# Centred tokens for the first gate chunks, earlier loads for slab 2, and a y tile between state inputs

## The chip, the cores and the metric

The kernel runs on one core of a Trainium2 chip. The time is device microseconds of that core for one execution; each version is run several times and its median is given. One more execution is taken with the hardware profiler, and everything called "the profile" or "the trace" comes from it.

The engines are named as the profile names them: PE (matrix products; PEld loads the stationary operand), DVE (vector operations), ACT (activation functions, also used to move results out of PSUM, the memory that PE writes to), POOL (here only powers and small copies) and SP (which issues nearly all DMAs, in order).

## What is computed

Tokens `x` (2048 of them, 512 channels, bf16) are layer-normalised. The normalised tokens feed two branches, a state space model with 512 complex states and a gated feed-forward network with 1376 hidden channels, and the branches are multiplied:

```python
xn = _layernorm(x, axis=-1)
# branch s: for each of 512 complex states
dt = jnp.exp(log_dt); Lam_bar = jnp.exp(dt * Lam)
B_bar = ((Lam_bar - 1.0) / Lam)[:, None] * Bmat
Bu = jnp.einsum("bld,pd->blp", xn + 0j, B_bar)
h = Lam_bar[None, :] * h + Bu[:, t, :]          # for t in range(2048)
s = 2.0 * jnp.einsum("blp,dp->bld", hseq, Cmat).real + xn * Dskip
# branch g
g = _silu((_gelu(xn @ w_gate) * (xn @ w_up)) @ w_down)
return x + s * g
```

## The kernel before, in words

**Tiling.** The 2048 tokens are four slabs (`s` = 0 to 3) of 512, each of four tiles (`m` = 0 to 3) of 128 tokens. A tile's normalised tokens `xn` must be turned (channels on the partitions) before PE can use them: `xnT`. For slab 0 PE turns them with an identity matrix (`head_t`, L427), and ACT (L430) or DVE (L432, tile 3) evicts the result; for the later slabs a DMA transpose does it (`dma_t`, L453).

**Work of a slab.** *Gate*: products of a tile with `wg` and `wu`, ACT takes Gelu of the one and copies the other, DVE multiplies them into `at`, and a DMA transpose turns that (`at_t`, L527). In slab 0 the weights come in three chunks of columns (`CH0`: 384, 512, 480), and `gate_pair` (L480 the products, L485 the copy `ub`, L486 the Gelu `gt`, L487 the product) takes one chunk of one tile; in the later slabs `gate_tile` (L501) takes a whole tile. *States*: `half(s, h)` has PE multiply the slab with two quarters of B (L612), ACT evicts to `U` (L615), and DVE rotates (L626, L634, L638), scans along time (L645) and rotates back into `hst`. *Down* (`down_pair`, L544): `atT` with `wd`, then ACT takes Silu into `g2` (L548). *y* (`y_tile`, L574): `hst` with `C2`, times `g2` (L578), plus the tokens (L586), stored to `out` (L589). The skip term `sk` (L457) is put into the y bank by ACT before the products (L570); for the first two y tiles only, DVE adds it behind the products instead (L582, L584).

**PSUM.** Three slots of two banks and two single banks (`ybank`). The gate pairs of chunk 0 take slots 0, 1, 2 and, for tile 3, both y banks; the first pair of chunk 1 is back at slot 0, so it must wait until pair 0 has been evicted by ACT.

**Order.** The steps are written down in a list (`Plan`), each with its engine, an estimated cost, the keys that it reads and writes, an earliest time and a rank. PE's order is the one written; DVE's is too while `in_turn` is set. For the other engines and queues a search (`run`) over orders of this list, with `TRIALS` random changes, takes the order that its estimates make shortest, and the instructions are issued in it. A wait on the chip comes from the keys alone. DMAs that are given with `dma_first` keep their order on their queue.

**The head, as it is written.** Stand-in products (`dummies`, L419, whose results nobody reads) run until there are tokens. Per tile of slab 0, DVE takes statistics (`stats`, L402), mean and variance (`mean`, L406), adds epsilon (`rstd`, L412), POOL raises that to -1/2 (`power`, L409), and DVE normalises (`norm_dve`, L444). In between, DVE makes the angles of the state tables (`angle`, L665 to L672). ACT loads its Sin table (L377) directly behind the Exp for `dt`, takes the two sines (L678, L679) and loads the Gelu table ahead of the first Gelu (L486). `spread` (L716, L717) copies Dskip to all partitions through slot 2, `damping` (L707) uses `ybank[0]`. SP's queue carries, in this order: tokens and weights of chunks 0 and 1, the tokens of slab 1 (L346), both parts of B turned (L348), the weights of chunk 2, `wd` (L753, L754), then slab 1's four turned tiles and both parts of C (L841; they land in `hst[1]`).

Of the kernel before, what the change touches and what calls it, by code (L numbers as in the profile page):

```python
# [19 lines left out]
LOOK, HOLD, TABLE, ROUNDS, TRIALS = 0.3, 8.0, 6.0, 6, 3000  # L20
# [182 lines left out]
def kernel(  # L203
# [50 lines left out]
    xnT = sb("xnT", [P, KT, 2 * TS])  # L254
# [20 lines left out]
    xn = [sb(f"xn{i}", [P, D]) for i in range(M)]  # L275
# [5 lines left out]
    tF = sb("tF", [P, 2, D], FP32)  # L281
    junk = sb("junk", [P, D])
# [31 lines left out]
    def dma_first(eng, issue, land, emit, writes, **kw):  # L314

        first[eng] = dma(eng, issue, land, emit, writes=writes, after=[first[eng]] if eng in first else (), **kw)
# [29 lines left out]
    dma_first(SP, 1.45, 4.0, lambda: nc.sync.dma_start(out=x_tok[:, M : 2 * M, :], in_=x_r[:, M : 2 * M, :]), [("x", 1, m) for m in range(M)])  # L346
    for ri, src in enumerate((A_B_re, A_B_im)):
        dma_first(SP, 2.4, 4.0, lambda ri=ri, src=src: nc.sync.dma_start_transpose(out=BT[:, ri, :, :], in_=src), [("BT", ri)])  # L348
    for which in range(2):
        load_w(dma_first, SP, nc.sync, 2, (1.35, 4.1), which)  # L350
# [21 lines left out]
    def columns():  # L372

        pe(1, 150, lambda: T.matmul(rows, lhsT=pv[0][:], rhs=ident[0 : 2 * NPT, 0 : 2 * NPT], start=True, stop=True),
            [("pv", 0), ("pv", 1), "ident"], [("slot", 2, 0)])
        acts(4, lambda: act(out=dt_, in_=rows[:, 0:NPT], func=AF.Exp), [("slot", 2, 0), "tiny"], ["dt"], table="exp", rank=150.0)
        acts(1, lambda: act(out=tiny[:], in_=zero[:], func=AF.Sin), ["zero", "dt"], ["tiny"], table="silu", rank=150.0)  # L377
# [44 lines left out]
    def transposed(src, n, dst, reads, writes, bank, evict):  # L422
        tp = ybank[bank][:].bitcast(BF16)[:, 0:D].rearrange("p (k t) -> p k t", t=P)

        def f():
            for k in range(KT):
                T.transpose(tp[:, k, :], src[:, k * P : (k + 1) * P], ident[:])  # L427
        pe(KT, P, f, reads + ["ident"], [("y", bank)])
        if evict == ACT:
            acts(512, lambda: act(out=dst, in_=tp, func=AF.Copy), [("y", bank)], writes, rank=100.0)  # L430
        else:
            dve(512, lambda: V.tensor_copy(out=dst, in_=tp), [("y", bank)], writes, rate=2.0, rank=40.0)  # L432
# [10 lines left out]
    def norm_dve(s, m):  # L443
        dve(512, lambda: V.tensor_scalar(  # L444
            out=xn[m][:], in0=x_tok[:, s * M + m, :], scalar1=mv[:, s, m, 0:1], scalar2=rs[:, s, m : m + 1],
            op0=ALU.subtract, op1=ALU.mult), [("x", s, m), ("mv", s, m), ("rs", s, m)], [("xn", m)], rate=2.0)

# [3 lines left out]
    def dma_t(s, m):  # L451
        c0 = (s % 2) * TS + m * P
        return dma(SP, 1.2, 4.5 if s == 1 else 1.3, lambda: nc.sync.dma_start_transpose(out=xnT[:, :, c0 : c0 + P], in_=xn[m][:]),  # L453
            [("xn", m)], turned_tile(s, m))

    def skip(s, m):
        dve(512, lambda: V.tensor_tensor(out=sk[s % 2][:, m, :], in0=xn[m][:], in1=Drow[:], op=ALU.mult),  # L457
            [("xn", m), "Drow"], [("sk", s % 2, m)], rate=2.0)
# [4 lines left out]
    def gate_pair(s, m, c, then=((), ()), spare=False):  # L463

        if spare:
            pss, both = [ybank[0][:], ybank[1][:]], [("y", 0), ("y", 1)]
        else:
            i, ps = slot()
            pss, both = [ps[:, 0, :], ps[:, 1, :]], [("slot", i, 0), ("slot", i, 1)]
        a, b = CH0[c]  # L470
        w = b - a
        j = (s * M + m) % NAT
        t0 = (s % 2) * TS + m * P
        q = gu_n[0] % (2 * NGT)
        gu_n[0] += 1
        qb, qo = q // 2, (q % 2) * 512
        for bank, (nm, wt) in enumerate((("wg", wg), ("wu", wu))):
            def f(bank=bank, wt=wt):
                for k in range(KT):
                    T.matmul(pss[bank][:, 0:w], lhsT=xnT[:, k, t0 : t0 + P], rhs=wt[:, k, a:b], start=(k == 0), stop=(k == KT - 1))  # L480
            pe(KT, w, f, turned_tile(s, m) + [(nm, c)], [both[bank]])
            for t in then[bank]:
                t()
        gd, ud = gt[qb][:, qo : qo + w], ub[qb][:, qo : qo + w]
        acts(w, lambda: act(out=ud, in_=pss[1][:, 0:w], func=AF.Copy), both, [("ub", q)])  # L485
        acts(w, lambda: act(out=gd, in_=pss[0][:, 0:w], func=AF.Gelu_apprx_tanh), both, [("gt", q)], table="gelu", after=early if c == 0 else (), rank=40.0 if c + m == 0 else 0.0)  # L486
        dve(w, lambda: V.tensor_tensor(out=at[j][:, a:b], in0=gd, in1=ud, op=ALU.mult), [("gt", q), ("ub", q)], [("at", j, c)], rate=2.0)  # L487

    def gate_tile(s, m):

        j = (s * M + m) % NAT
        t0 = (s % 2) * TS + m * P
# [3 lines left out]
        def mm(ps, bank, wt, c):  # L496
            a, b = CH[c]

            def f():
                for k in range(KT):  # L500
                    T.matmul(ps[:, bank, 0 : b - a], lhsT=xnT[:, k, t0 : t0 + P], rhs=wt[:, k, a:b], start=(k == 0), stop=(k == KT - 1))  # L501
# [51 lines left out]
    def y_tile(s, m):  # L553
        i = y_n[0] % 2
        seed = y_n[0] >= 2
# [7 lines left out]
        for bank, key, a, z in parts:  # L563
            y_part(s, m, bank, key, a, z, i, e, gi, b, seed)

    def y_part(s, m, bank, key, a, z, i, e, gi, b, seed):

        w = z - a
        if seed:
            acts(w, lambda: act(out=bank, in_=sk[s % 2][:, m, a:z], func=AF.Copy), [("sk", s % 2, m)], [key])  # L570

        def f():
            for j in range(2 * NPT):
                T.matmul(bank, lhsT=hst[s % 2][:, j // NPT, j % NPT, m * P : (m + 1) * P], rhs=C2[:, j // NPT, j % NPT, a:z],  # L574
                         start=(j == 0 and not seed), stop=(j == 2 * NPT - 1), skip_group_check=True)
        pe(2 * NPT, w, f, [("hst", s % 2, 0), ("hst", s % 2, 1)] + C2S + ([key] if seed else []), [key])
        if seed:
            dve(w, lambda: V.tensor_tensor(out=yg[e][:, a:z], in0=bank, in1=g2[gi][:, b, a:z], op=ALU.mult),  # L578
                [key, ("g2", gi)], [("yg", e, a)], base=0.13)
        else:  # L580
            ys = tF[:, i, :]
            dve(512, lambda: V.tensor_tensor(out=ys, in0=bank, in1=sk[s % 2][:, m, :], op=ALU.add),  # L582
                [key, ("sk", s % 2, m)], [("tF",)], base=0.13)
            dve(512, lambda: V.tensor_tensor(out=yg[e][:], in0=ys, in1=g2[gi][:, b, :], op=ALU.mult),  # L584
                [("tF",), ("g2", gi)], [("yg", e, a)], base=0.13)
# [16 lines left out]
    def half(s, h):  # L602

        ui = u_n[0] % NU
        u_n[0] += 1
        for q in range(H2):
            i, ps = slot()
            pt = h * H2 + q
            for ri in range(2):
                def f(ri=ri, pt=pt, ps=ps):  # L610
                    for k in range(KT):
                        T.matmul(ps[:, ri, :], lhsT=BT[:, ri, k, pt * P : (pt + 1) * P], rhs=xnT[:, k, (s % 2) * TS : (s % 2 + 1) * TS],  # L612
# [3 lines left out]
                 [("slot", i, 0), ("slot", i, 1)], [("U", ui, q)])  # L616
        WQ = [P, 2, 2, H2 * TS]
# [56 lines left out]
    def tables():  # L674
# [3 lines left out]
        early.append(acts(196, lambda: act(out=sbt[:], in_=ang[:], func=AF.Sin, scale=TWO_PI), ["ang"], ["sbt"], table="silu", rank=20.0))  # L678
        early.append(acts(196, lambda: act(out=cbt[:], in_=kr[:], func=AF.Sin, scale=-TWO_PI, bias=halfpi[:]), ["kr", "halfpi"], ["cbt", "trig"], table="silu", rank=20.0))  # L679
        for f32, lo, pr, n in ((cbt, ch, cp, "c"), (sbt, sh, sp, "s")):  # L680
            pool(0.5, lambda f32=f32, lo=lo: G.tensor_copy(out=lo[:], in_=f32[:, :, 0:NB]), [n + "bt"], [n + "h"])
            acts(128, lambda f32=f32, pr=pr: act(
                out=pr[:], in_=f32[:, :, NB : NB + NA].unsqueeze(3).to_broadcast([P, NPT, NA, 2]), func=AF.Copy), [n + "bt"], [n + "p"], rank=40.0)
# [28 lines left out]
    def head_t(m):  # L712
        transposed(xn[m], m, xnT[:, :, m * P : (m + 1) * P], [("xn", m)], [("xnT", 0, m)], m % 2, DVE if m == 3 else ACT)

    def spread():
        pe(1, 512, lambda: T.matmul(slots[2][:, 1, :], lhsT=warm[0:1, 0:P], rhs=Drow[0:1, :], start=True, stop=True), ["Drow", "warm"], [("slot", 2, 1)])  # L716
        acts(512, lambda: act(out=Drow[:], in_=slots[2][:, 1, :], func=AF.Copy), [("slot", 2, 0), ("slot", 2, 1)], ["Drow"])  # L717
# [3 lines left out]
    dummies(3, 0)  # L721
# [3 lines left out]
    rstd(0, 0, 1)  # L725
    stats(0, 1)
    mean(0, 1)
    norm_dve(0, 0)
    rstd(0, 1, 2)
    head_t(0)  # L730
    dummies(2, 0, 3)
    turn_angles()
    angle(0)
    norm_dve(0, 1)
    stats(0, 2)
    mean(0, 2)
    rstd(0, 2, 3)
    angle(1)
    stats(0, 3)
    norm_dve(0, 2)  # L740
    mean(0, 3)
    rstd(0, 3, 4)
    angle(2)
    angle(3)
    norm_dve(0, 3)
    pl.in_turn = False
    tables()
    then = {0: ((lambda: head_t(1), spread), ()), 1: ((lambda: head_t(2),), ()), 2: ((lambda: head_t(3),), ())}
    for m in range(M):
        gate_pair(0, m, 0, then.get(m, ((), ())), m == M - 1)  # L750
        if m == 1:
            damping()
    dma_first(SP, 3.6, 4.3, lambda: nc.sync.dma_start(out=wd[:, 0 : NFT - 1, :], in_=B_w_down[0 : (NFT - 1) * P, :].rearrange("(k p) d -> p k d", p=P)), ["wd"])  # L753
    dma_first(SP, 0.4, 4.3, lambda: nc.sync.dma_start(out=wd[:FL, NFT - 1, :], in_=B_w_down[(NFT - 1) * P : F, :]), ["wd"])  # L754
    for m in range(M):
        skip(0, m)
    for m in range(M):
        gate_pair(0, m, 1)
    for h in range(2):
        half(0, h)  # L760
    for m in range(M):
        gate_pair(0, m, 2)
# [38 lines left out]
    turned = {}  # L801

# [108 lines left out]
```

## Time and profile before

| what | us |
|---|---|
| median of 5 runs (lowest to highest) | 181.02 (180.85 to 181.15) |
| profiled execution | 181.15 |
| its span, first to last instruction | 179.4 |
| around the span | 1.75 |
| PE busy (share) | 173.5 (97%) |
| DVE busy | 158.1 (88%) |
| ACT busy | 117.4 (65%) |
| POOL busy | 9.7 (5%) |

Times inside the profile count from the first instruction. PE's products overlap, so one of 512 columns stands with 379 ns while the next starts 216 ns after it; PE's busy share says that it always had one under way, and the start of the products is what to read. The same holds for ACT and DVE on a smaller scale: an eviction of 384 columns stands with 0.49 us, and the next starts 0.37 us after it. Some records of products are missing from a trace, which leaves a hole of one product.

The profile's strip of 40 slices shows when each engine works; a digit is the busy share in tenths:

```profile
PE   7999999999999999999999999999999999999992
...
DVE  3889999999999999999999999999999999950063
ACT  4788599699999998645369964426618666353220
```

After the first slice PE is never below nine tenths until the end.

### The profile page before, as it was taken

The page shows a single profiled execution, that of the slowest core. Times are in us where ns is not written, and L with a number is a line of the kernel's source. Part 1 is how long each engine was busy: PE and PEld are TensorE (multiplying, and loading weights), DVE is VectorE, ACT ScalarE, POOL GpSimd, SP SyncE. Part 2 cuts the span into 40 slices and gives each one's busy share as a digit, 9 for nine tenths or more (in the row PEclk, how much of TensorE's full clock was granted, in tenths as well). Part 3 has the DMA queues.
Part 4 walks back from the last instruction along what each step waited for, and adds up shares of the span by engine and source line. Part 5 has one row for each costly group of instructions (what it writes and reads, how often), then busy time and mean ns, then how long its engine had stood idle before and what let it go on. Part 6 is the DMA issues. An engine that isn't in the chain of part 4 may idle for free.

```text
span 179.4 us, 2392 instructions
## 1 busy us (share of the span) xinstructions
PE 173.5 (97%) x838; PEld 82.6 (46%) x854; DVE 158.1 (88%) x268; ACT 117.4 (65%) x178; POOL 9.7 (5%) x19
## 2 busy tenths in 40 slices
PE   7999999999999999999999999999999999999992
PEld 2454444444445545444445554544445555444451
DVE  3889999999999999999999999999999999950063
ACT  4788599699999998645369964426618666353220
POOL 3330230000002000000020000000000000000000
PEclk9999999999999999999999999999999999999999
DMA  5999999994000456620011575050100084420011
GB/s 141 295 315 220 360 203 214 274 220 87 0 0 0 80 97 90 127 48 0 0 60 62 104 146 109 0 111 4 58 29 0 2 161 84 89 79 29 0 58 59
DMA packets 47109, 18.01 MB, mean 100 GB/s; under 512 B 38425, under 2 KB 47098, under 8 KB 47098
## 3 DMA queue, kind: packets, MB, share of 16 engines
q1 hardware_dynamic: 47072, 17.86, 44.2%
q8 instruction: 6, 0.10, 0.2%
q14 instruction: 5, 0.04, 0.1%
q10 hardware_dynamic: 26, 0.00, 0.0%
HBM read 6.33 MB, written 2.10 MB: 47 GB/s over the span
## 4 chain that ended last, share of the span: by engine, by line
PE 91%; DMA 4%; DVE 1%; SPq 1%; issue 1%; DVEq 0%
PE slot L501 31%; PE slot L544 21%; PE slot L612 15%; PE ybank L574 13%; PE slot L480 9%; DMA wu<-in_B_w_up_dram 3%; DMA out_dram<-ot 1%; PE ybank L480 1%; DVE ot L586 1%; SPq L328 1%; DVE yg L578 1%; PE ybank L427 0%; SPq L321 0%; PE ybank L707 0%; DVEq L586 0%
## 5 line engine op out<-in xcount | busy, mean ns | idle before, releaser
L501 PEld LDWEIGHTS <-xnT 128*128 128x128 bf16 x288 | 28.2, 98 | 28.4
L544 PE MATMUL slot<-wd,atT 128*128 128x512 bf16 (+1 forms) x173 | 38.5, 379 | 0.2
L501 PE MATMUL slot<-wu,xnT 128*128 128x512 bf16 (+1 forms) x144 | 31.8, 357 | 0.0
L501 PE MATMUL slot<-wg,xnT 128*128 128x512 bf16 (+1 forms) x139 | 31.5, 356 | 0.3
L645 DVE TENSOR_TENSOR_SCAN Fs<-rho,ini,W 128x512 bf16<-128x512 f32 x24 | 29.3, 1266 | 0.0
L612 PE MATMUL slot<-xnT,BT 128*128 128x512 bf16 x124 | 28.1, 379 | 0.2
L574 PE MATMUL ybank<-C,hst 128*128 128x512 bf16 (+1 forms) x125 | 27.6, 372 | 0.2
L544 PEld LDWEIGHTS <-atT 128*128 128x128 bf16 (+1 forms) x176 | 17.2, 98 | 20.9
L615 ACT ACTIVATE U<-slot 128x1024 bf16<-128x1024 f32 x16 | 16.1, 1021 | 12.7 <-PE slot L612 12.6
L578 DVE TENSOR_TENSOR yg<-ybank,g 128x512 bf16<-128x512 f32 (+1 forms) x14 | 9.4, 669 | 12.9 <-PE ybank L574 12.5
L574 PEld LDWEIGHTS <-hst 128*128 128x128 bf16 x136 | 13.3, 98 | 13.8
L612 PEld LDWEIGHTS <-BT 128*128 128x128 bf16 x128 | 12.5, 98 | 15.1
L626 DVE TENSOR_TENSOR Q<-U,tab 128x4096 bf16<-128x4096 bf16 x8 | 18.3, 2287 | 0.2
L626 DVE TENSOR_TENSOR Q<-Fs,tab 128x4096 bf16<-128x4096 bf16 x8 | 18.3, 2286 | 0.1
L548 ACT ACTIVATE g<-slot 128x1024 f32<-128x1024 f32 x8 | 8.2, 1024 | 13.5 <-PE slot L544 13.5
L570 ACT ACTIVATE ybank<-sk 128x512 f32<-128x512 bf16 (+1 forms) x14 | 8.1, 585 | 11.8 <-DVE yg L578 11.5
L509 ACT ACTIVATE gt<-slot 128x1024 bf16<-128x1024 f32 x12 | 12.3, 1023 | 4.2 <-PE slot L501 4.2
L509 ACT ACTIVATE ub<-slot 128x1024 bf16<-128x1024 f32 x12 | 12.3, 1022 | 3.9 <-PE slot L501 3.7
L480 PEld LDWEIGHTS <-xnT 128*128 128x128 bf16 x96 | 9.1, 98 | 9.7 <-ACT xnT L430 0.7
L480 PE MATMUL slot<-wg,xnT 128*128 128x480 bf16 (+2 forms) x43 | 10.4, 360 | 0.4 <-ACT xnT L430 0.4
L480 PE MATMUL slot<-wu,xnT 128*128 128x512 bf16 (+2 forms) x44 | 10.4, 360 | 0.1
L823 ACT ACTIVATE junk<-x_tok 128x512 bf16<-128x512 bf16 x16 | 10.0, 624 | 0.5 <-DMA x_tok<-in_A_x_dram 0.3
(118 smaller groups left out, 178.5 us busy)
## 6 DMA issues: line engine op xcount, KB each, us to landing
out_dram<-ot SPq DMA_DIRECT2D x15, 128.0 KB, 1.7
x_tok<-in_A_x_dram SPq DMA_DIRECT2D x3, 512.0 KB, 4.9
wd<-in_B_w_down_dram SPq DMA_DIRECT2D x1, 1280.0 KB, 9.3
x_tok<-in_A_x_dram SPq DMA_DIRECT2D x4, 128.0 KB, 3.0
wg<-in_B_w_gate_dram SPq DMA_DIRECT2D x1, 512.0 KB
wu<-in_B_w_up_dram SPq DMA_DIRECT2D x1, 512.0 KB, 6.8
wg<-in_B_w_gate_dram SPq DMA_DIRECT2D x1, 480.0 KB, 4.6
wu<-in_B_w_up_dram SPq DMA_DIRECT2D x1, 480.0 KB
```

The costliest lines, as they stand in the source:

```text
L480: T.matmul(pss[bank][:, 0:w], lhsT=xnT[:, k, t0 : t0 + P], rhs=wt[:, k, a:b], start=(k == 0), stop=(k == KT - 1))
L501: T.matmul(ps[:, bank, 0 : b - a], lhsT=xnT[:, k, t0 : t0 + P], rhs=wt[:, k, a:b], start=(k == 0), stop=(k == KT - 1))
L509: acts(1024, lambda ps=ps, dst=dst, fn=fn: act(out=dst[:, 0:1024].rearrange("p (c w) -> p c w", c=2), in_=ps[:, :, :], func=fn), [("slot", ...
L544: T.matmul(ps[:, b, :], lhsT=atT[:fs, k, m * P : (m + 1) * P], rhs=wd[:fs, k, :], start=(k == 0), stop=(k == NFT - 1))
L548: acts(1024, lambda: act(out=g2[gi][:, :, :], in_=ps[:, :, :], func=AF.Silu), [("slot", i, 0), ("slot", i, 1)], [("g2", gi)], table="silu" ...
L574: T.matmul(bank, lhsT=hst[s % 2][:, j // NPT, j % NPT, m * P : (m + 1) * P], rhs=C2[:, j // NPT, j % NPT, a:z], start=(j == 0 and not seed ...
L578: dve(w, lambda: V.tensor_tensor(out=yg[e][:, a:z], in0=bank, in1=g2[gi][:, b, a:z], op=ALU.mult), [key, ("g2", gi)], [("yg", e, a)], base ...
L612: T.matmul(ps[:, ri, :], lhsT=BT[:, ri, k, pt * P : (pt + 1) * P], rhs=xnT[:, k, (s % 2) * TS : (s % 2 + 1) * TS], start=(k == 0), stop=(k ...
L615: acts(1024, lambda q=q, ps=ps: act(out=U[ui][:, :, q, :], in_=ps[:, :, :], func=AF.Copy), [("slot", i, 0), ("slot", i, 1)], [("U", ui, q)])
L626: dve(4096, lambda: V.tensor_tensor(out=Qf, in0=src.unsqueeze(1).to_broadcast(WQ), in1=table, op=ALU.mult), reads, ["Q"], rate=2.0)
L645: pl.add(DVE, 1.116 if s == 0 else 1.19, lambda ri=ri, q=q, pt=pt, first=first: V.tensor_tensor_scan(out=Fs[:, ri, q, :], data0=rho[:, pt ...
L823: acts(512, lambda i=i, fn=fn, m=m: act(out=junk[:], in_=x_tok[:, s * M + m, :], func=fn, accum_out=sx[:, s, i, m : m + 1]), [("x", s, m)] ...
```

## The change

- In slab 0, DVE only takes the mean off a tile (`center`) and PE turns this; it lies in `xcT`, an alias of `W`, while `xc` is an alias of `Fs`. The gate products of chunks 0 and 1 (`bare`) use it, and ACT multiplies by the token's 1/sigma (`scale=rs`) in the copy and in the Gelu of a pair. Powers on POOL are taken for two tiles at once. The tokens are normalised afterwards as before, and one DMA transpose (`turn_slab`) turns all of slab 0 for chunk 2 and the states.
- `xnT` is two tensors, one for odd and one for even slabs, with the tile ahead of the channel block. The states' products so read four runs of 128 columns.
- Chunk 0's products are put in another order on PE: gate of tile 0, spread, gate of tile 1, up of tile 0, and so on. The stand-ins are 6, 1 and 2 of 512 columns, where they were 6, 3 of 512 and 2 of 384.
- ACT's Sin table load comes behind the eviction of tile 1 (`behind`).
- SP's queue: B turned, slab 0 turned, slab 1's tokens, chunk 2's weights, the first part of C, slab 1 turned in one transpose, `wd`, the second part of C.
- The loads of slab 2's and slab 3's tokens get a rank of 40 in the search, and slab 3's may come from 50.0 us on by its estimates, where it was 30.0.
- All y tiles are seeded by ACT. The last y tile ahead of a slab's state inputs stands between the two halves' inputs (`inputs`, `states`).
- `TRIALS` is 8000.

```diff
-LOOK, HOLD, TABLE, ROUNDS, TRIALS = 0.3, 8.0, 6.0, 6, 3000
+LOOK, HOLD, TABLE, ROUNDS, TRIALS = 0.3, 8.0, 6.0, 6, 8000
...
-    xnT = sb("xnT", [P, KT, 2 * TS])
+    xnT = [sb(f"xnT{i}", [P, M, KT, P]) for i in range(2)]
...
+    xc = [Fs[:, i // 2, i % 2, :] for i in range(M)]
+    xcT = W[:].rearrange("p r q t -> p (r q t)").rearrange("p (m k t) -> p m k t", m=M, k=KT)
...
-    dma_first(SP, 1.45, 4.0, lambda: nc.sync.dma_start(out=x_tok[:, M : 2 * M, :], in_=x_r[:, M : 2 * M, :]), [("x", 1, m) for m in range(M)])
-    for ri, src in enumerate((A_B_re, A_B_im)):
-        dma_first(SP, 2.4, 4.0, lambda ri=ri, src=src: nc.sync.dma_start_transpose(out=BT[:, ri, :, :], in_=src), [("BT", ri)])
-    for which in range(2):
-        load_w(dma_first, SP, nc.sync, 2, (1.35, 4.1), which)
+    def load_rest():
+        for ri, src in enumerate((A_B_re, A_B_im)):
+            dma_first(SP, 1.9, 5.0, lambda ri=ri, src=src: nc.sync.dma_start_transpose(out=BT[:, ri, :, :], in_=src), [("BT", ri)])
+        first[SP] = turn_slab(0, 3.5, [first[SP]])
+        dma_first(SP, 1.45, 3.5, lambda: nc.sync.dma_start(out=x_tok[:, M : 2 * M, :], in_=x_r[:, M : 2 * M, :]), [("x", 1, m) for m in range(M)])
+        for which in range(2):
+            load_w(dma_first, SP, nc.sync, 2, (1.35, 3.5), which)
+        load_c(0)
...
+    def turn_slab(s, land, after=()):
+        return dma(SP, 2.0, land, lambda: nc.sync.dma_start_transpose(
+            out=xnT[s % 2][:].rearrange("p m k t -> p (m k) t"), in_=xn_all[:].rearrange("p m d -> p (m d)")),
+            [("xn", m) for m in range(M)], [("xnT", s % 2, m) for m in range(M)], after=after)
...
+    def center(m):
+        dve(512, lambda: V.tensor_scalar(out=xc[m], in0=x_tok[:, m, :], scalar1=mv[:, 0, m, 0:1], scalar2=None, op0=ALU.subtract),
+            [("x", 0, m), ("mv", 0, m)], [("xc", m)], rate=2.0)
...
+            src = xcT if self.bare else xnT[0]
...
+            if self.bare:
+                kw, rd, ptr = dict(scale=rs[:, 0, m : m + 1]), [("rs", 0, m)], 1
+            up = acts(w, lambda: act(out=ud, in_=pss[1][:, 0:w], func=AF.Copy, **kw), self.both + rd, [("ub", q)], ptr=ptr)
+            gelu = acts(w, lambda: act(out=gd, in_=pss[0][:, 0:w], func=AF.Gelu_apprx_tanh, **kw), self.both + rd, [("gt", q)], table="gelu", ptr=ptr,
+                 after=[*early, up] if c + m == 0 else (), rank=60.0 if c + m == 0 else 0.0)
...
-                    T.matmul(ps[:, ri, :], lhsT=BT[:, ri, k, pt * P : (pt + 1) * P], rhs=xnT[:, k, (s % 2) * TS : (s % 2 + 1) * TS],
+                    T.matmul(ps[:, ri, :], lhsT=BT[:, ri, k, pt * P : (pt + 1) * P], rhs=xnT[s % 2][:, :, k, :],
...
     dummies(6, 0)
     columns()
-    dummies(3, 0)
+    dummies(1, 0)
     pl.in_turn = True
     stats(0, 0)
     mean(0, 0)
-    rstd(0, 0, 1)
+    center(0)
     stats(0, 1)
     mean(0, 1)
...
+    center(1)
+    rstd(0, 0, 2)
     turn_angles()
     angle(0)
...
+    center(3)
+    rstd(0, 2, 4)
+    norm_dve(0, 0)
+    pl.in_turn = False
+    head_t(0, ACT)
+    dummies(2, 0)
+    behind = [head_t(1, ACT)]
+    acts(1, lambda: act(out=tiny[:], in_=zero[:], func=AF.Sin), ["zero", "dt"], ["tiny"], table="silu", rank=60.0, after=behind)
+    sines()
+    pairs = [GatePair(m, 0, m == M - 1) for m in range(M)]
+    pairs[0].products(0)
+    spread()
+    pairs[1].products(0)
+    pairs[0].products(1)
+    head_t(2, ACT)
+    pairs[1].products(1)
+    damping()
+    pairs[2].products(0)
+    pl.in_turn = True
+    head_t(3, DVE)
+    norm_dve(0, 1)
+    norm_dve(0, 2)
     norm_dve(0, 3)
     pl.in_turn = False
-    tables()
...
+    pairs[2].products(1)
+    pairs[3].products(0)
+    pairs[3].products(1)
+    gelus = [p.close() for p in pairs]
+    tables(gelus[:1])
+    load_rest()
...
         for m in range(M):
             norm_dve(1, m)
-            turned[1] = dma_t(1, m)
+        first[SP] = turn_slab(1, 3.0, [first[SP]])
+        for m in range(M):
             skip(1, m)
...
-            writes=[("x", s, m) for m in range(M)], not_before=30.0)
+            writes=[("x", s, m) for m in range(M)], not_before=(30.0, 50.0)[s - 2], rank=40.0)
...
         if not last:
-            for m in range(M - late, M):
-                y_tile(s - 1, m)
-                skip(s + 1, m)
+            for h, tiles in enumerate((range(M - late, M - 1), range(M - 1, M))):
+                for m in tiles:
+                    y_tile(s - 1, m)
+                    skip(s + 1, m)
+                inputs(s + 1, h)
             for h in range(2):
-                half(s + 1, h)
+                states(s + 1, h)
```

## The prediction

> **What bounds the kernel now.** I read the page first: busy shares and the chain of work that ended last.
>
> ```profile
> PE 173.5 (97%) x838; PEld 82.6 (46%) x854; DVE 158.1 (88%) x268; ACT 117.4 (65%) x178; POOL 9.7 (5%) x19
> ...
> PE 91%; DMA 4%; DVE 1%; SPq 1%; issue 1%; DVEq 0%
> ```
>
> PE holds the chain. The table of waits gives PE two waits in all: 1.1 us for the first memset and 0.4 us for xnT. The chain in order of time has only PE pieces (and 0.05 us ones of issue) from 7.76 to 172.38 us, so the products stand wall to wall. The tail (last y tile, product by g2, sum with x, one store) is not edited. So only the head can give time: what counts is when PE comes to its unbroken run, the first product of gate chunk 1. The timeline shows how PE gets there:
>
> ```profile
> 4.16 0.57 POOL L409 TENSOR_TENSOR rs<-ve,mhalf 128x1 f32<-128x1 f32 x1 [2.11 <-DVE ve L412]
> ...
> 4.81 0.38 DVE L444 TENSOR_SCALAR xn<-x_tok,mv,rs 128x512 bf16<-128x512 bf16 x1
> ...
> 5.25 0.40 PE L427 MATMUL ybank<-ident,xn 128*128 128x128 bf16 x4
> ...
> 5.68 0.60 ACT L430 ACTIVATE xnT<-ybank 128x512 bf16<-128x512 bf16 x1
> ...
> 6.33 0.82 PE L480 MATMUL slot<-wg,xnT 128*128 128x384 bf16 x4 [0.36 <-ACT xnT L430]
> ...
> 7.76 0.81 PE L480 MATMUL slot<-wu,xnT 128*128 128x384 bf16 x4
> 8.40 0.81 PE L480 MATMUL slot<-wg,xnT 128*128 128x384 bf16 x4
> ...
> 13.19 1.03 PE L480 MATMUL slot<-wg,xnT 128*128 128x512 bf16 x3
> ```
>
> Tile 0 goes variance, power on POOL, normalise, transpose, evict, product. The up product waits until 7.76, and the chain names its releaser: a DMA that no edit touches.
>
> ```profile
> 2.74 4.97 DMA wu<-in_B_w_up_dram
> 7.71 0.04 issue
> 7.76 1.46 PE slot L480 x8
> ```
>
> **The start.** Centring needs the mean alone, so it starts where ve did (3.92) and not at 4.81. By the nearest row (L444, 0.38) it ends at 4.30. Stand-ins run at 0.43 us apiece until 5.25, about half the later pace (0.216 for 512 columns), so I give the transposes 0.2 more: eviction 5.0 to 5.6. wg chunk 0 lands 3.9 after its issue at 1.65, that is 5.55. Tile 1: statistics from 4.22 (0.73), aggregate (0.21), centred 5.54, transposed from 5.60, evicted about 6.63. PE: transposes, gate 0 (5.83 to 6.48), spread (0.22), gate 1 (6.75 to 7.40), and then the up weights at 7.71 as before. One pair of halves has been moved ahead of that wait: gate 1.
>
> **The sum.** From 7.76 to 13.19 PE now does seven products of 0.65 (4.55), two sets of transposes at 0.24 (0.48), damping (0.09) and 0.31 of short waits: 5.43. Afterwards six products remain: 3.90 + 0.48 + 0.09 + 0.31 = 4.78, and chunk 1 starts at 12.54. **Gain 0.65 us.** Both ends: nothing, if the gates only shift the wait; 0.65 + 0.31 = 0.96, if the short waits go too. I take 0.65, because the waits have a heir: damping writes the bank that tile 2's eviction reads (about 9.45, PE free at 9.30).
>
> **ScalarE must be through too.** Chunk 1 reuses slot 0, so pair 0 must be closed. The Sin table load loses its cover:
>
> ```profile
> 4.14 1.28 ACT L377 ACT_TABLE_LOAD   x1
> ...
> 10.33 0.45 ACT L679 ACTIVATE cbt<-kr,halfpi 128x196 f32<-128x196 f32 x1
> 10.79 1.28 ACT L486 ACT_TABLE_LOAD   x1
> 12.08 0.49 ACT L486 ACTIVATE gt<-slot 128x384 bf16<-128x384 f32 x1
> ```
>
> At 4.14 it filled idle time; now it is put behind tile 1's eviction. By start-to-start times: from 6.53, load and tiny 1.48, Drow 0.49, eviction of tile 2 0.50, sines 0.26 + 0.46, up 0.37, Gelu load 1.29, Gelu 0.49: 11.87. Queued behind the load are Drow and tile 2's eviction, for which PE's damping and gate 2 wait. A scale pointer costs half of L804's surplus over L430 (0.812 - 0.597): 0.11. Two of them give 12.09, which is 0.45 ahead of PE. All 16 early evictions gain 1.7 us; what hides it is ACT's idle time before ub at 16.85, 18.57 and 20.30 (0.62 + 0.64 + 0.64). If that cover is gone, slots come free later, at most 0.7 in sum.
>
> The Trainium skill speaks against this move: "ScalarE: Activation LUTs", section "What ACT_TABLE_LOAD costs", counts a drain of about 1.38 us on top of each load. Here the load starts 0.01 after the sine and Gelu 0.01 after the load; with that drain twice, an estimate from that page, pair 0 would close at about 14.9 and the kernel would lose 1.7 us. The trace decides, so I leave the drain out.
>
> **DVE, POOL.** Four centrings add 4 x 0.38 = 1.5; the first two y tiles lose their sum in tF (2 x 0.69 = 1.4) and put two seeds of 0.60 on ACT. DVE is full from 15 us on, so even is what it needs. Four powers of 0.57 become two of width 2, between 0.57 and 1.12 each, and are needed only by the closing of a pair.
>
> **Stand-ins.** Three of 512 after the columns become one, two of 384 become two of 512. PE's work for the clock is about as dense. If full clock came later, gates 0 and 1 would run at half and end by about 8.7: up to 1 us.
>
> **Moving operand.** The state inputs read xnT in four runs of 128 columns. The stand-ins of 384 re-read a 128-column block and take the 326 ns of plain 384 products: 0. Upper bound by the transposes (0.23 for four of 128, against 0.216): 128 x 0.014 = 1.8. I take 0; a read in blocks is the nearer row.
>
> **SP's queue.** The load of slab 1 moves behind both B transposes and a new transpose of all of slab 0:
>
> ```profile
> 5.83 6.45 SPq L348 DMA_TRANSPOSE BT<-in_A_B_re_dram  x1
> 12.33 2.11 SPq L348 DMA_TRANSPOSE BT<-in_A_B_im_dram  x1
> ```
>
> B_re was held until 12.28 by the transfers ahead; without 512 KB (about 1.5 us at 300 GB/s and more) B_im ends near 13.0. The normalised tokens are ready near 12.1. The new transpose issues 13.0 to 15.1 and lands, by C_re's 4.8 from issue, near 17.8; by B_re's 8.7, at 21.7. PE wants it at 13.19 - 0.65 + 6.9 = 19.4. I take 17.8, since C_re had a short queue ahead as well. Behind it wait slab 1's tokens (about 20, after 4.9), wg and wu chunk 2 (wanted at 26.3), C_re, slab 1's transpose (tokens normalised about 26.5, landing 31, wanted 32.8) and wd (before: 9.3 to land; wanted at 39.7). DVE covers the later tokens with table products (6 x 1.22). Each has 1.5 us or more, so nothing is charged.
>
> **Slabs 2 and 3.** Tokens loaded at another time, and a y tile put between the inputs, leave PE's work the same; no PE wait stands there, so nothing is to be gained. The nearest loss is one seed (0.60) or one product for at (0.68) that comes ahead of what PE waits for: 0 to 0.7; I take 0, since PE found none late before.
>
> **Rivals.**
> 1. ScalarE takes the place of the up weights. If tile 2's eviction comes after the sines (0.72) and a wait for angles is added, pair 0 closes about 12.8, chunk 1 starts about 12.95: gain 0.2, 180.8. For it: ACT 4.97 of 5.00 us in 10 to 15. Against: 0.45 in hand.
> 2. Slower: slab 0's turned tokens. Place: the first state input at 19.4. Price: one for one. Point: it must land after 20.4 to use up the gain and 0.36. At B_re's 8.7 from issue PE stands 2.3 us: 181.02 - 0.65 + 2.3 = 182.7; midway about 181.6. For it: the transfer queue carries 200 GB/s and more until 22 us. Against: 512 KB less ahead.
> 3. The early products give nothing because the weights bind anyway: were wu late by 0.65 too, 181.0. No edit delays it.
> 4. Half clock until gates 0 and 1 end: 181.3 to 181.4, by the 1 us above.
>
> **Numbers.** The profiled execution took 181.15, its span 179.4, 1.75 around it. Minus 0.65: 180.50. The median of the runs is 0.13 lower, 181.02, so 180.4. Chances: forecast 0.64 (its own range 180.0 to 180.65), rivals 1 and 3 together 0.16, rival 2 0.17, rival 4 0.03. What this measurement can tell from no change is about 0.2%, 0.36 us. Faster 0.64, same 0.16, slower 0.20. The range 179.95 to 181.4 takes in the forecast and rivals 1, 3 and 4, and leaves out most of rival 2.
>
> **What would show it.** Right: first gate product near 5.8, up product of pair 0 still at 7.7 to 7.8, chunk 1 at 12.4 to 12.7, no PE wait from there, DVE's work within 0.5 us. Wrong: a PE wait at the first state input or at slab 1's, a chain that holds ACT between 6.5 and 12.5, an L612 product slower than 0.216 start to start, or stand-ins at 0.43 after 5.5.

## The result, and the profile after

| | before | after |
|---|---|---|
| median, us (lowest to highest) | 181.02 (180.76 to 181.6, 50 runs) | 180.51 (179.91 to 182.71, 28 runs) |
| profiled execution, its span | 181.15, 179.4 | 180.81, 179.0 |
| first gate product of tile 0 | 6.33 | 5.65 |
| first up product | 7.76 | 7.80 |
| first product of chunk 1 | 13.19 | 12.48 |
| first state input | 20.10 | 19.39 |
| first product with `wd` | 40.39 | 39.68 |
| first gate product of slab 1 | 49.91 | 49.61 |
| last product | 175.56 | 175.26 |

The ratio of the medians is 0.997, with a 95% interval of 0.9963 to 0.9977: 0.51 us less by the medians (0.3%). The run of 182.71 counts as slow and is not in the ratio. The table's lower rows are starts in the two profiled executions and show where the time comes from. At chunk 1 the changed kernel is 0.71 ahead, and it keeps that for 27 us. Between the first product with `wd` and slab 1 it loses 0.41, and from there to the last product the two run in step.

The page of the changed kernel, its busy times and the shares of its chain by engine:

```profile
PE 173.2 (97%) x838; PEld 82.5 (46%) x852; DVE 157.8 (88%) x268; ACT 119.2 (67%) x180; POOL 7.9 (4%) x17
...
PE 69%; DVE 17%; DMA 7%; ACT 3%; issue 1%; SPq 1%; DVEq 0%
```

PE's busy time is what it was (173.5 before). That its share of the chain drops from 91% to 69% looks dramatic, but means one thing only: the chain is followed back from the end, and at one place, 47.2 us, it leaves PE because PE waited there. Everything earlier is then laid to the work that led to that wait. The table of PE's waits says how much is behind it:

```profile
PE slot L437 <- DVE zero L381: 1.1, 1, 1.1
PE slot L501 <- DMA wu<-in_B_w_up_dram: 0.3, 1, 0.3
PE slot L573 <- DMA atT<-at: 0.2, 1, 0.2
```

The head, in the timeline (start, duration, what; in brackets the idle time before it and its releaser):

```profile
3.80 0.35 DVE L466 TENSOR_SCALAR Fs<-x_tok,mv 128x512 bf16<-128x512 bf16 x1
...
4.91 0.60 ACT L448 ACTIVATE W<-ybank 128x512 bf16<-128x512 bf16 x1 [0.79 <-PE ybank L445]
...
5.65 0.81 PE L501 MATMUL slot<-wg,W 128*128 128x384 bf16 x4
...
6.71 0.82 PE L501 MATMUL slot<-wg,W 128*128 128x384 bf16 x4
...
7.80 0.81 PE L501 MATMUL slot<-wu,W 128*128 128x384 bf16 x4 [0.26 <-DMA wu<-in_B_w_up_dram]
...
10.54 1.28 ACT L514 ACT_TABLE_LOAD   x1
...
11.84 0.58 ACT L514 ACTIVATE gt<-slot,rs 128x384 bf16<-128x384 f32 x1
12.48 1.03 PE L501 MATMUL slot<-wg,W 128*128 128x512 bf16 x3
```

The first tile is centred at 3.80, a whole microsecond before it was normalised (4.81). Two gate groups, 5.65 and 6.71, are now done when the up weights come, where there was one. The up product itself starts where it did. ACT begins pair 0's Gelu at 11.84 and its next instruction at 12.32, and the Gelu's own record ends at 12.42. Slot 0 is free when PE comes for it, and chunk 1 at 12.48 is set by PE, not by ACT: the four products ahead of it (from 11.83) and it stand wall to wall.

The place where time is given back, in the queue of SP:

```profile
31.25 7.98 SPq L556 DMA_TRANSPOSE atT<-at  x3
39.29 2.21 SPq L362 DMA_TRANSPOSE hst<-in_A_C_im_dram  x1
41.59 1.60 SPq L556 DMA_TRANSPOSE atT<-at  x1
```

and in the chain of waits (start, duration, what):

```profile
41.59 5.58 DMA atT<-at
47.22 2.55 PE slot L573 x11
```

Slab 0's fourth turned tile of `at` stands in the queue behind the second part of C. It is issued at 41.59, takes 5.58 to land, and PE has nothing to do until 47.22. From the first product with `wd` to slab 1 PE takes 9.93 us where it took 9.52. These 0.41 are from start to start; the table of waits counts 0.2, from the recorded end of the product before.

### The profile page after: what moved, and what is told of

Same layout as the page of the kernel before. It is cut to its first block, busy times and chain, and to the rows that moved or that the text cites. A ratio compares the mean times of both kernels' runs of the same rounds, so it can differ in the third digit from the quotient of the medians.

```text
span 179.0 us, 2387 instructions
## 1 busy us (share of the span) xinstructions
PE 173.2 (97%) x838; PEld 82.5 (46%) x852; DVE 157.8 (88%) x268; ACT 119.2 (67%) x180; POOL 7.9 (4%) x17
## 3 DMA queue, kind: packets, MB, share of 16 engines
HBM read 6.33 MB, written 2.10 MB: 47 GB/s over the span
## 4 chain that ended last, share of the span: by engine, by line
PE 69%; DVE 17%; DMA 7%; ACT 3%; issue 1%; SPq 1%; DVEq 0%
PE slot L530 30%; PE slot L573 17%; PE ybank L601 13%; PE slot L638 8%; DMA atT<-at 3%; DVE Q L656 3%; DMA wu<-in_B_w_up_dram 3%; DVE Fs L675 3%; DVE Q L725 3%; DVE at L516 2%; DVE st L420 1%; DVE tab L725 1%; DMA out_dram<-ot 1%; DVE sk L473 1%; DVE ot L606 1%
## 5 line engine op out<-in xcount | busy, mean ns | idle before, releaser
L530 PEld LDWEIGHTS <-xnT 128*128 128x128 bf16 x288 | 28.2, 98 | 28.4
L638 PE MATMUL slot<-xnT,BT 128*128 128x512 bf16 x128 | 28.6, 379 | 0.0
L604 DVE TENSOR_TENSOR yg<-ybank,g 128x512 bf16<-128x512 f32 (+1 forms) x16 | 10.7, 668 | 12.8 <-PE ybank L601 12.6
L656 DVE TENSOR_TENSOR Q<-U,tab 128x4096 bf16<-128x4096 bf16 x8 | 18.3, 2286 | 0.3
L656 DVE TENSOR_TENSOR Q<-Fs,tab 128x4096 bf16<-128x4096 bf16 x8 | 18.3, 2286 | 0.1
L597 ACT ACTIVATE ybank<-sk 128x512 f32<-128x512 bf16 (+1 forms) x16 | 9.3, 585 | 9.2 <-DVE yg L604 9.2
L675 DVE TENSOR_TENSOR_SCAN Fs<-rho,W 128x512 bf16<-128x512 f32 x8 | 9.2, 1206 | 0.0
L501 PEld LDWEIGHTS <-W 128*128 128x128 bf16 x64 | 5.9, 98 | 6.0 <-issue 0.5
L548 DVE TENSOR_TENSOR at<-gt,ub 128x1024 bf16<-128x1024 bf16 x12 | 8.2, 684 | 0.4 <-ACT ub L538 0.2
```

The costliest lines, as they stand in the source:

```text
L530: T.matmul(ps[:, bank, 0 : b - a], lhsT=xnT[s % 2][:, m, k, :], rhs=wt[:, k, a:b], start=(k == 0), stop=(k == KT - 1))
L548: dve(1024, lambda: V.tensor_tensor(out=at[j][:, 0:1024], in0=gt[q][:, 0:1024], in1=ub[q][:, 0:1024], op=ALU.mult), qs[0] + qs[1], [("at", ...
L656: dve(4096, lambda: V.tensor_tensor(out=Qf, in0=src.unsqueeze(1).to_broadcast(WQ), in1=table, op=ALU.mult), reads, ["Q"], rate=2.0)
L675: pl.add(DVE, 1.116 if s == 0 else 1.19, lambda ri=ri, q=q, pt=pt, first=first: V.tensor_tensor_scan(out=Fs[:, ri, q, :], data0=rho[:, pt ...
```

## The experiments

Two questions were open. **In the head**: is the gain what the prediction named, gate 1 put into the wait for the up weights, or is it the earlier start that centring brings, or the order alone? **Further on**: is the 0.41 at 47 us the queue's fault, and are the other moved transfers free? Every experiment made from the changed kernel has the order of its steps, as the search had found it, written down as a list, so that an edit moves only the rows it names and nothing is searched anew. The ratios are to the kernel before on the same chip (181.01 to 181.05). In the diffs a row is an instruction by the profile's name and line.

### e1_c_im_early: C's second part out of the way

```diff
 L362 hst<-in_A_C_re_dram
+L362 hst<-in_A_C_im_dram
 L366 xnT<-xn (slab 1)
...
 L556 atT<-at x3
-L362 hst<-in_A_C_im_dram
 L556 atT<-at
```

> The changed kernel with its order held fixed, and one DMA moved: the transpose of C's imaginary part is issued right behind the real part's, ahead of slab 1's turn, so that the fourth turned tile of at no longer stands behind it on SP's queue. Theory (the head gives 0.71 us, and 0.41 of it goes back into a PE wait at 47 us for that tile): the wait goes, the last product of PE starts 0.65 to 0.75 earlier than before, and the time is 180.1 to 180.35. Rival (the wait stood in the one profiled execution, or the transfers themselves are late, whatever the order): PE still waits at 47 us or elsewhere, 180.5.

Measured: 180.15 (179.91 to 180.78), ratio to before 0.9958 (0.9942 to 0.9973). The queue of SP:

```profile
23.90 2.31 SPq L362 DMA_TRANSPOSE hst<-in_A_C_im_dram  x1
...
32.00 9.40 SPq L556 DMA_TRANSPOSE atT<-at  x4
```

The four turns now go out one behind the other, and PE has no wait at 47 us: 9.51 from the first product with `wd` to slab 1. The fourth tile lands 3.87 us after its issue (39.78 to 43.65), where it took 5.58. That the transpose of C stood in the way is shown. What it is worth in time is not: the interval overlaps that of the changed kernel, so it was run again below. The last product starts 0.95 earlier than before, more than expected: in this execution the up weights landed at 7.03, and chunk 1 began at 12.04.

### e2_up_first: e1 with up of tile 0 ahead of gate of tile 1

```diff
 pairs[0].products(0)
 spread()
-pairs[1].products(0)
 pairs[0].products(1)
+pairs[1].products(0)
```

> e1 with two groups of PE swapped back: the up product of tile 0 again ahead of the gate product of tile 1; centring stays. Theory (the gain is one pair of products moved into the wait for the up weights, which land at 7.7 whatever is done): chunk 1 starts 0.6 to 0.7 later than in e1, near 13.1, and the time is 0.65 above e1, 180.8 to 181.0. Rival (the gain is that centring starts the products 0.7 earlier): as e1, 180.2.

Measured: 180.54 (180.12 to 180.97), 0.9971 (0.9961 to 0.9982), less of a loss than expected. The profiled execution tells why: here the trace's semaphore events have the up weights landed at 6.78. The up product starts at 7.06 and chunk 1 at 12.41. There was no wait to move gate 1 into. Against e1 the order costs 0.2 to 0.4, with intervals that overlap; the 0.65 of the prediction isn't in it.

### e3_before_gate_first: the kernel before with that order alone

```diff
 head_t(1)
 spread()
+gate of tile 1, chunk 0
 up of tile 0, chunk 0
-gate of tile 1, chunk 0
```

> The kernel before with its order held fixed and the same two groups of PE swapped: gate of tile 1 ahead of up of tile 0, without centring. Theory: tile 1 is evicted at 8.02 only, so gate 1 starts at 8.05 and up 0 after it; chunk 1 starts at 13.2 to 13.4, the time is 181.0 to 181.25. Rival (the order alone is the gain, centring is not needed): chunk 1 at 12.6, 180.4.

Measured: 181.61 (181.42 to 181.9), 1.0032 (1.0021 to 1.0043): slower than before. PE's timeline:

```profile
8.27 0.82 PE L480 MATMUL slot<-wg,xnT 128*128 128x384 bf16 x4 [0.37 <-ACT xnT L430]
8.93 0.81 PE L480 MATMUL slot<-wu,xnT 128*128 128x384 bf16 x4
...
13.78 1.03 PE L480 MATMUL slot<-wg,xnT 128*128 128x512 bf16 x4
```

Without centring, tile 1 is evicted too late for its gate product, PE waits 0.37 for it, and up of tile 0, whose weights had landed at 7.00, comes at 8.93. The rival that the order alone brings the gain falls. The loss, 0.59 at chunk 1, is larger than expected; the medians agree with it (181.61 against 181.05). A part of it is not the order's: full clock came at 6.65 in this execution and at 5.25 in the first one of the kernel before, and the first gate product started at 6.46 instead of 6.33.

### e4_sin_first: e1 with the Sin table loaded ahead of the first eviction

```diff
+L779 tiny (Sin table)
 L448 W<-ybank (tile 0)
 L448 W<-ybank (tile 1)
-L779 tiny (Sin table)
```

> e1 with ACT's Sin table load put back ahead of the first eviction, where it was before. Theory (the weights that land at 7.7 set the pace, not the first product's start nor ACT): the first gate product starts near 6.3 in place of 5.65, up of tile 0 still at 7.8 to 7.9, chunk 1 within 0.1 of e1, the time within 0.15 of e1, 180.1 to 180.45. Rival (the early start itself is worth its 0.7): 180.8 to 181.0.

Measured: 180.52 (180.51 to 180.87), 0.9976 (0.9967 to 0.9986). The first gate product comes at 6.17, where e1 has 5.63, and PE then waits for the eviction:

```profile
PE slot L501 <- ACT W L448: 0.3, 1, 0.3
```

The up weights landed at 7.49, but up starts at 7.91 and chunk 1 at 12.60. So in this execution a late start is not swallowed by a wait for the weights, as the prediction's picture would have it. With weights as late as in the next run (7.88) it would be: chunk 1 begins at 12.61 there, although its first gate product starts at 5.75. The time lies between what the two theories gave.

### again_after: the changed kernel once more

> The changed kernel itself, once more, for a second profile and for times beside the others of this set. Theory (the up weights of chunk 0 land anywhere from 6.8 to 7.8 us from one execution to the next, and the PE wait for them is that of one execution; the wait at 47 us for the fourth turned tile belongs to the order of SP's queue and so comes each time): a PE wait at 47 us of 0.2 to 0.6 again, the up product of tile 0 at 7.3 to 7.8, 180.5. Rival (the wait at 47 us is chance): no such wait, 180.1 or less in this profile.

Measured: 180.31 (180.12 to 180.65), 0.9961 (0.9949 to 0.9974). The wait for the up weights is there again (0.3, weights at 7.88); the wait at 47 us is not: 9.53 from `wd` to slab 1. It is missed by a hair: the fourth turned tile lands at 46.89, 5.51 us after its issue, and PE comes for it at 46.94. In the first profile the tile landed at 47.17 and PE could have started at 46.82. So the late landing goes with the order of SP's queue, and whether PE waits for it differs from one execution to the next.

### e5_loads_as_before: e1 with the tokens of slabs 2 and 3 where they were

```diff
 L894 wd<-in_B_w_down_dram
+L872 x_tok<-in_A_x_dram x2 (slabs 2 and 3)
 L556 atT<-at x4
...
-L872 x_tok<-in_A_x_dram (slab 2 ahead of the last part of wd, slab 3 behind the turns)
```

> e1 with the tokens of slabs 2 and 3 issued one behind the other ahead of the turned tiles of at, as in the kernel before. Theory (SP's queue ahead of the first down product is what the loads' place decides): the 512 KB more ahead of the first turned tile push its landing back by about 1.5 us from 36 to 38, to the 39.3 where PE wants it; PE waits there 0 to 0.8 us and the time is 180.15 to 180.9. Rival (the loads' place has no part): no PE wait, 180.15.

Measured: 181.05 (180.71 to 182.13), 1.0008 (0.9993 to 1.0022): the whole gain is gone. SP's queue and PE's waits:

```profile
31.04 1.41 SPq L872 DMA_DIRECT2D x_tok<-in_A_x_dram  x2
32.55 11.44 SPq L556 DMA_TRANSPOSE atT<-at  x4
```

```profile
PE slot L573 <- DMA atT<-at: 1.4, 1, 1.4
```

In the profile before, both loads stood at that place too, and PE waited for no turned tile. With the new order of the queue ahead of them, the turns land too late by 1.4 us when both loads go first. That is more than the 0 to 0.8 expected, and it is the reading of one execution, the slowest of the twelve (182.13). By the medians their move has a value of 0.75 to 0.9 us (181.05 less e1's 180.3, see below, and 180.15), which the prediction had at nothing.

### e6_y_tile_ahead: e1 with slab 2's y tile ahead of both inputs

```diff
+L601 ybank<-C,hst x8 (with its seed L597, and L604)
 L638 slot<-xnT,BT x16
-L601 ybank<-C,hst x8
 L638 slot<-xnT,BT x16
```

> e1 with slab 2's y tile put back ahead of both halves' inputs, its seed and the product that frees its bank moved ahead with it. Theory (PE had no wait at this place before and has none now, so the tile's place is worth nothing to the time): within 0.15 of e1, 180.0 to 180.3. Rival (the later tile is what gives DVE its inputs early enough): a PE wait behind 70 us, 180.5 or more.

Measured: 180.37 (180.25 to 180.78), 0.9968 (0.9955 to 0.998). PE has a hole of 0.31 at 72.87 that e1 doesn't have. Against e1's two medians that is 0.1 to 0.2, which these intervals can't tell from nothing.

### e7_spread_early: e1 with the one-row product ahead of tile 1's transposes

```diff
+L748 slot<-Drow,junk
 L445 ybank<-ident,Fs (tile 1)
 L501 slot<-wg,W (tile 0)
-L748 slot<-Drow,junk
...
 L448 W<-ybank (tile 0)
+L749 Drow<-slot
 L448 W<-ybank (tile 1)
```

> e1 with the product that spreads Dskip put ahead of tile 1's transposes, where PE only runs stand-ins, and its eviction between those of tiles 0 and 1. Theory (in most executions the up weights are there in time, and the products stand wall to wall from the first gate product on, so that each 0.1 us taken out ahead of chunk 1 counts): chunk 1 0.25 to 0.32 earlier where the weights land by 7.0, 179.85 to 180.05. Rival (the up weights or ACT's closing of pair 0 bind): as e1, 180.15.

Measured: 181.05 (180.48 to 182.3), 1.0015 (0.999 to 1.004), and the times fall in two groups: seven from 180.48 to 181.18, five from 182.03 to 182.30. The profiled execution belongs to the second. PE's timeline:

```profile
6.20 0.60 PE L445 MATMUL ybank<-ident,Fs 128*128 128x128 bf16 x4
6.60 2.77 PE L501 MATMUL slot<-wg,W 128*128 128x384 bf16 x8
9.16 1.09 PE L501 MATMUL slot<-wu,W 128*128 128x384 bf16 x4
```

Eight products of 384 columns take 2.56 from start to start of the next group, 0.32 each, twice the usual 0.16. PE runs at half its pace until about 9.7. The page's clock column says full clock for every slice, but the trace's record of the granted clock only begins at 9.70 and has nothing ahead of that; the pace has to be read from the starts. The expected gain doesn't show in the other group either: its median is 180.56, above e1's 180.15, and it left no profile that could tell why.

### e9_c_im_again: e1 once more

> e1 once more, for its times beside the changed kernel on one chip. Theory (with the fourth turned tile no longer behind C's transpose on SP's queue no execution waits for it, where some of the changed kernel's do): 180.0 to 180.3, 0.1 to 0.4 below the changed kernel, no PE wait behind 10 us. Rival (the move gains nothing beyond chance): within 0.1 of the changed kernel.

Measured: 180.3 (180.0 to 180.82), 0.9966 (0.9955 to 0.9977). No wait at 47 us. The head, with the up weights landed at 7.17:

```profile
5.81 0.81 PE L501 MATMUL slot<-wg,W 128*128 128x384 bf16 x4
...
6.87 0.82 PE L501 MATMUL slot<-wg,W 128*128 128x384 bf16 x4
7.53 0.81 PE L501 MATMUL slot<-wu,W 128*128 128x384 bf16 x4
...
12.22 0.38 PE L501 MATMUL slot<-wg,W 128*128 128x512 bf16 x1
```

Nothing is waited for between the gate products and the up product: 6.87 + 4 x 0.16 is 7.51.

### e10_after_third: the changed kernel beside it

> The changed kernel a third time, beside e1 on one chip. Theory: 180.3 to 180.6; a PE wait at 47 us in this profile or not, as the first profile had 0.41 us and the second none. Rival: as e1.

Measured: 180.34 (179.94 to 181.26), 0.9971 (0.9958 to 0.9985), on the same chip as e9. There is a hole of 0.12 at 47.19, where the fourth turned tile landed at 47.15, 5.58 after its issue. The head differs from e9's, although the up weights were early here too (7.21):

```profile
5.95 1.20 PE L501 MATMUL slot<-wg,W 128*128 128x384 bf16 x4
7.08 0.39 PE L748 MATMUL slot<-Drow,junk 1*128 1x512 bf16 x1
...
12.74 1.03 PE L501 MATMUL slot<-wg,W 128*128 128x512 bf16 x3
```

The trace's record of full clock begins at 6.72 (5.63 in e9), tile 0's gate group takes 1.13 up to the next product (0.74 in e9), and chunk 1 comes 0.52 later.

Moving C's second part takes the wait at 47 us away in each profile, but 0.04 between the medians is nothing: the rival, that it gains no time that can be told, stands.

### e11_fewer_stand_ins: e1 without two stand-ins

```diff
 L445 ybank<-ident,Fs (tile 0)
-L437 slot<-junk x2
 L445 ybank<-ident,Fs (tile 1)
```

> e1 without the two stand-in products behind tile 0's transposes, so that PE stands idle from about 4.7 to 5.4. Theory (the clock is released at the end of a stretch that was full enough, at 4.1 to 6.2 us, and a stretch with less in it is passed over, as in e7, whose products ran at half pace until 9.7): part of the executions at 180.1 to 180.5, part at 181.8 to 182.4, as e7's were; stand-ins are what keeps it. Rival (e7 was slow for another reason): all executions at 180.0 to 180.5.

Measured: 181.11 (179.97 to 182.38), 1.0005 (0.9976 to 1.0034): six executions from 179.97 to 180.47 and six from 181.74 to 182.38. The profiled one, again of the second group:

```profile
4.24 0.63 PE L445 MATMUL ybank<-ident,Fs 128*128 128x128 bf16 x4
5.43 0.61 PE L445 MATMUL ybank<-ident,Fs 128*128 128x128 bf16 x4 [0.56 <-DVE Fs L466]
5.83 1.49 PE L501 MATMUL slot<-wg,W 128*128 128x384 bf16 x4
7.25 0.60 PE L748 MATMUL slot<-Drow,junk 1*128 1x512 bf16 x1
7.79 1.46 PE L501 MATMUL slot<-wg,W 128*128 128x384 bf16 x4
9.04 1.27 PE L501 MATMUL slot<-wu,W 128*128 128x384 bf16 x4
```

PE is idle for 0.56 where the two products were, and the gate groups take 1.42 and 1.25 up to the next product, where they take 0.74 and 0.66 in e9. The record of full clock begins at 9.96, and chunk 1 starts at 14.19. Nothing else in the kernel was touched. So it is shown that the two stand-ins keep the slow group away: none of e1's 17 executions took over 180.82, and six of twelve do here. By what measure the clock judges PE's work is not shown.

### e12_before_again: the kernel before once more

> The kernel before, for a second profile of it. Theory (the weights' landing varies between executions and the PE wait for them at 7.7 us is that of the first profile; when they come early the kernel before is bound by its chain of normalising, transposing and evicting): where the up weights land by 7.2, the up product of tile 0 starts at 7.5 to 7.6, right behind the spread, and chunk 1 at 12.9 to 13.1; where they land at 7.7 again, as in the first profile, 7.8 and 13.2. Rival (the landing is fixed by the order of the loads): 7.7 again.

Measured: 181.12 in the one profiled execution, with a span of 179.0; 2.1 us lie around it, where 1.75 did in the first profile, so the two times agree although the spans differ by 0.4. The up weights landed at 6.73:

```profile
6.21 0.82 PE L480 MATMUL slot<-wg,xnT 128*128 128x384 bf16 x4 [0.36 <-ACT xnT L430]
...
7.19 0.39 PE L716 MATMUL slot<-Drow,junk 1*128 1x512 bf16 x1
7.51 0.82 PE L480 MATMUL slot<-wu,xnT 128*128 128x384 bf16 x4
...
12.86 0.81 PE L480 MATMUL slot<-wg,xnT 128*128 128x512 bf16 x2
```

The up product follows the spread at once. The wait until 7.76, on which the prediction's sum was built, was that of one execution of the kernel before.

## Why the prediction was right, and where it was not

**Size and place.** 180.4 was given, 180.51 measured; 0.65 of gain was given, 0.51 measured. It comes from the head, and the products stand wall to wall behind it but for 0 to 0.41 us at 47. First gate product 5.65 (given 5.83), up product 7.80 (given 7.71 and after), chunk 1 at 12.48 (given 12.54).

**The named cause holds for some executions only.** The prediction said that "a DMA that no edit touches" holds the up product, and that moving gate 1 ahead of this wait is the gain. The up weights' landing was read in every profile: between 6.73 and 7.91, in one and the same kernel too (7.71 and 6.73 before; 7.76, 7.88 and 7.21 after). PE waited for it only where it was 7.7 and later. In most of the others the head is an unbroken row of products from the first gate product on, and what counts is when that row starts, how long it is and when full clock comes. Seven profiled executions have the changed kernel's head (its own three, e1, e5, e6 and e9). With late weights chunk 1 begins at 12.48, 12.61 and 12.63 (13.19 before); with early ones at 12.04, 12.09 and 12.22 (12.86 before), and at 12.74 in e10, where the clock was late. Before (e12) against e9, both with early weights, shows what the gain is made of: start 6.21 to 5.81, and from there to chunk 1 6.65 to 6.41, since tile 1's transposes (0.31 before) are already done when the first gate product starts. That sums to 0.64 (12.86 to 12.22). With late weights the first pair of profiles gives 0.71. So the gain at chunk 1 is 0.56 to 0.71 by the prediction's way and 0.64 to 0.82 by the other, but 0.12 with e10's late clock. With one execution of the kernel before on each side these are readings and not measured means. That the other way comes out near 0.65 too is luck: the prediction had not worked it out.

Gate 1's move is not the larger part: with it put back behind the up product the median is still 0.51 below the kernel before (e2). Centring is needed for the new order, which loses 0.59 at chunk 1 without it (e3); centring alone was not run. How the rest divides between the order (e2) and the place of the Sin load (e4) stays open; each is 0.2 to 0.4 by the medians against e1 and its repeat, with overlapping intervals.

**ScalarE.** Pair 0's Gelu was given to end at 12.09 for the next instruction and did at 12.32, 0.16 ahead of PE instead of 0.45; it is 0.16 or 0.17 in e1, e6, e9 and both repeats of the changed kernel too. Rival 1 did not come about, but was nearer than it looked. The pointer's surcharge was given as 0.11; copies of 384 columns stand with 0.57 to 0.58 where they had 0.49. The load at 10.54 ends at 11.82 and Gelu starts at 11.84. The drain of about 1.38 us that the Trainium skill, "ScalarE: Activation LUTs", section "What ACT_TABLE_LOAD costs", puts on each load is not in this trace either, with 0.02 in its place.

**DVE, POOL, moving operand.** DVE 158.1 to 157.8, POOL 9.7 to 7.9, as given. A state input of 16 products takes 3.45 us in the changed kernel's chain, 0.216 each: the four runs of 128 columns cost nothing.

**SP's queue: terms mis-sized or missing.** "Each has 1.5 us or more" was too wide: slab 0's turn was given to land at 17.8 and landed at 18.3 with the first state input at 19.39, so 1.1 was in hand, and in the other profiles 0.3 at the least. Rival 2 was near. The second part of C and the turned tiles of `at` around it are not in the prediction's list; the fourth tile had nothing in hand (0.05 us in the second profile, a wait of 0.41 and 0.12 in the others). And on the loads of slabs 2 and 3 the step "no PE wait stands there" with "I take 0" failed: it was read from the old queue. In the new one (as e1 has it) their place is not free: put back, they cost 0.75 to 0.9 (e5). Their move brings nothing against the kernel before; it keeps a wait away that the rest of the new order would make.

**Rival 4 was under-weighted.** "PE's work for the clock is about as dense" was too sure: in one of the changed kernel's three profiles full clock came late enough to cost 0.5 at chunk 1 (e10 against e9), and the margin to worse is two stand-ins. Without them half of the executions lose 1.7 us (e11), and a one-row product moved ahead does the same in five of twelve (e7).

**The best version** is e1 with 180.15 and 180.3, against 180.34 for the changed kernel beside it: not a difference that can be told.

## What to carry to other kernels

A transfer's landing in one profile is one draw: before a wait of a few tenths is made the base of a sum, ask what the sum is when the transfer is early, and trust the number only if it comes out alike. An edit that moves a transfer is to be costed in the queue as it will be, not as it was; "nobody waits there now" holds only for the old order. Fill PE's first microseconds with products of full width, because a stretch that is too thin may cost far more (here 1.7 us) than the work that was saved.

## What the runs showed of the hardware

- **Full clock comes at different times.** The trace's record of the granted clock begins between 3.75 us (e1) and 6.72 us (e10) in twelve of the fourteen profiled executions (5.25 and 4.58 before; 5.04, 4.34 and 6.72 in the changed kernel), and at 9.70 and 9.96 in e7 and e11, whose second groups take 1.7 us more. The starts agree: in e7, e10 and e11 products of 384 columns stand 0.32 apart ahead of it and 0.16 behind it.
- The Trainium skill, "TensorE: Matmul & The Clock Gate", section "🔬 Part 1: The HAM clock gate (the "warmup" mystery)", has activity judged in windows of about 3.4 us that run freely, not from the kernel's start, with full clock after one busy window. The traces agree on the length: the recorded stretch of full clock is 174.08 us in eleven of them, 170.67 in e7 and e11 and 177.49 in e5, which is 51, 50 and 52 times 3.413. That it doesn't run from the kernel's start fits the spread above. By this step e7 and e11 were passed over at about 6.29 and 6.55 (an estimate: 9.70 and 9.96 less 3.41). What share of a window must be busy, no run here shows.
- **The same load lands 1.2 us apart.** 384 KB of up weights, issued at 2.73 to 2.75, landed between 6.73 and 7.91.
- **A transpose lands later behind another one.** Slab 0's fourth tile of `at` landed 5.5 to 5.6 us after its issue in the three profiles of the changed kernel, where C's second part was issued just ahead of it, and after 3.8 to 4.0 in the eight profiles made from it, where the third tile was.
